# Seven-product pairs of blocks without GpSimd: products in another order, summed in PSUM over copies, in operations twice as wide

## The chip, the cores and the metric

The kernel runs on one core of a Trainium2 chip. The metric is the device time of one execution in microseconds (us), shown as the median of several runs. One execution was also taken by the hardware profiler; where the text says "the profiled execution", it means that one.

## The reference

All inputs are float32; B = 8 sequences, 8 heads, S = 576 positions, 64 features per head, so rows of 512 features. What is computed, cut to what matters:

```python
kv  = einsum('bhsd,bhse->bhde', k, v)          # per head, 64 x 64
out = einsum('bhsd,bhde->bhse', q, kv)         # linear attention without softmax
x   = out / sqrt(mean(out**2, -1) + 1e-6) * g_norm     # then heads side by side: [8, 576, 512]
u   = x + ((x^T @ U) @ V)^T                    # U [576, 32], V [32, 576]: mixes positions
y   = u + relu(u @ w_ch1) @ w_ch2              # [512, 2048] and [2048, 512]
```

U, V and the two large weights come as float64 and are decoded to float32 on the chip.

## The kernel before

**Blocks.** The 8 x 576 = 4608 rows of u are held transposed and cut into nine blocks of 512 columns. Blocks 0 to 2 go through the two large products directly: for each of 16 chunks f of the 2048 hidden features, `ffn1` makes one 128x512 tile h, `relu` makes its two parts hh and hl, and `ffn2` adds into four PSUM banks y. To keep float32 accuracy on the fast matmul, every operand is split into a high part (a rounding copy, on ScalarE) and a low part (source minus high part, on VectorE); a product is three matmuls, high by high, high by low, low by high.

**Pairs.** Blocks 3 to 8 go as three pairs (q = 0, 1, 2). A pair is a 2x2 block problem, done with seven products P1 to P7 instead of eight. `UNITS` lists 112 units of six 128x512 matmuls for each pair: 28 units of a *first stage* (`first_unit`: four groups g of h, seven products each), 28 units of a *second stage* (`second_unit`: seven products, four units each, summing over g), and the same again for the other half of the hidden features. So a pair has four stages, first, second, first, second, and there are twelve stages in all.

**What feeds the stages.** `factor` makes the right-hand operands of the first stage (sums and differences of blocks, then split). `weight_combos` makes the weights of all seven products during blocks 1 and 2, 16 calls in all, and puts them in DRAM (`wd`), from where `load_units` fetches four units at a time. In the first stage the sums of P1, P6 and P5 are copied to SBUF (`spare`, L635), P7, P3, P4 and P2 are added to them on VectorE (L638) and rectified on ScalarE (L639), and GpSimd makes the combinations of h that the second stage needs (L641, L642, L662, L664). In the second stage `make_part` splits a combination into hh (ScalarE, L659) and hl (VectorE, L660) up to three units ahead of the unit that uses it; the results are added to x on VectorE (L693, L695) and, from the copies, on GpSimd (L689). GpSimd also does the sums inside `weight_combos` (L571, L579) and the differences in `factor` (L545).

**Attention beside it.** While PE works on one block or pair, the attention of later sequences is prepared in steps of one head pair each: `kv_step`, `out_step`, `stats_step`, `mul_step`, `xsplit_step`, `turn_step`, `t_step`, `t4_step`, `mix_part`. `STARTS`, `PARTS`, `STARTS2` and `EARLY` say behind which unit each step stands.

**Order.** PE's order is that of the program from block 2 on; before that, and on the other engines throughout, a scheduler places the instructions when the program is built. Every engine takes its queue in order. All DMAs are issued by SyncE (SP).

Of the kernel before, what the change touches and what calls it, by code (L numbers as in the profile page):

```python
# [82 lines left out]
def build(ctx: ExitStack, tc: tile.TileContext, kv_in, kvt0_in, kvt_in, q_in, uv_in, g_in, w_in, out):  # L83
# [152 lines left out]
    def decode_w(f):  # L236
# [9 lines left out]
        def low_half():  # L246
            w = got["w"]
            nc.vector.tensor_tensor(out=w[:, 1], in0=t, in1=w[:, 0].bitcast(F32), op=ALU.subtract)
# [16 lines left out]
    def bank():  # L265
        bank_no[0] += 1
        if startup[0] and bank_no[0] % (7 - NEARLY) >= 3 - NEARLY:
            return ps_y.tile([P, 512], F32, name="y")
        return ps_p.tile([P, 512], F32, name="pp")

    def low_bank(b):
        return ps_h.tile([P, 512], F32, name="h") if b > 4 else bank()
# [862 lines left out]
```

## Time and profile before

| what | value |
|---|---|
| time, median of 3 runs | 924.05 us (923.7 to 924.52) |
| profiled execution, its own time | 923.1 us |
| span of its instructions | 921.1 us |
| busy, TensorE (PE) | 864.7 us, 94% |
| busy, VectorE (DVE) | 671.2 us, 73% |
| busy, ScalarE (ACT) | 463.1 us, 50% |
| busy, GpSimd (POOL) | 357.8 us, 39% |
| first matmul of the pairs | at 374.3 us |

PE, DVE, ACT, POOL and SP are TensorE's matmuls, VectorE, ScalarE, GpSimd and SyncE; PEld is TensorE's loading of weights. A row of a group reads: line, engine, operation, output and inputs, shapes, count, then busy time in us and the mean of one in ns, then how long the engine sat idle before such instructions and what ended that. A matmul counts as busy for its whole latency, so a PE that is busy is not one at its peak.

### The profile page before, as it was taken

To read this page: it belongs to the slowest core of one execution; us is meant where nothing else is said; L and a number is where in the kernel's file an instruction comes from. 1 tells how busy PE (TensorE), PEld (TensorE's weight loads), DVE (VectorE), ACT (ScalarE), POOL (GpSimd) and SP (SyncE) were. 2 spreads that over 40 slices of the span, in tenths; PEclk is the share of its full clock that TensorE was granted. 3 is DMA by queue.
4 is the path that set the end of the run, shared out by engine and by line. 5 is a ranking of instruction groups with operands and counts; after the bars stand their busy time and mean duration, and the time that the engine had idled before them with its cause. 6 is when DMAs were issued, how large, how long until landed. Compare 5 with 4: busy or idle time off the path is not lost.

```text
span 921.1 us, 12302 instructions
## 1 busy us (share of the span) xinstructions
PE 864.7 (94%) x4196; PEld 704.4 (76%) x4196; DVE 671.2 (73%) x1099; ACT 463.1 (50%) x890; POOL 357.8 (39%) x301
## 2 busy tenths in 40 slices
PE   8899998989979999999899969998999699999998
PEld 7678876878868888887688747787887478878876
DVE  5798877666688566679786997369659973484496
ACT  5677733433334244455545835455457434553553
POOL 2000037566553002134242692137325932543491
PEclk9999999999989999999899989999999999999999
DMA  9989865535666462377568536765566367555553
GB/s 344 418 317 293 244 191 191 191 118 199 193 204 193 124 204 94 132 248 276 171 210 294 199 118 194 262 234 170 201 221 209 97 199 253 185 187 201 204 186 133
DMA packets 76670, 191.17 MB, mean 208 GB/s; under 512 B 8640, under 2 KB 38848, under 8 KB 65856
## 3 DMA queue, kind: packets, MB, share of 16 engines
q1 hardware_dynamic: 76608, 190.39, 61.3%
q8 instruction: 33, 0.54, 0.2%
q14 instruction: 29, 0.24, 0.1%
HBM read 143.30 MB, written 47.05 MB: 207 GB/s over the span
## 4 chain that ended last, share of the span: by engine, by line
PE 47%; DVE 17%; DMA 2%; issue 2%; ACT 1%; SPq 0%; POOL 0%; DVEq 0%; ACTq 0%
PE y L629 18%; PE y L678 15%; PE y L489 4%; DVE dec L660 4%; DVE hl L660 4%; DVE uc L554 2%; PE pp L312 2%; DVE hk L638 1%; PE pp L289 1%; PE h L475 1%; PE h L476 1%; PE h L477 1%; DMA out<-x 1%; DVE x L693 1%; DVE xt L370 1%
## 5 line engine op out<-in xcount | busy, mean ns | idle before, releaser
L629 PE MATMUL y<-uc,wt 128*128 128x512 f32 x966 | 229.9, 393 | 1.0 <-ACT sp L635 1.0
L629 PEld LDWEIGHTS y<-uc,wt 128*128 128x128 f32 x966 | 178.7, 188 | 37.9 <-ACT sp L635 1.4
L678 PE MATMUL y<-dec,wt 128*128 128x512 f32 x504 | 128.8, 399 | 1.4 <-DVE dec L660 0.7
L678 PEld LDWEIGHTS y<-dec,wt 128*128 128x128 f32 x504 | 94.2, 191 | 27.9 <-DVE dec L660 9.0
L489 PE MATMUL y<-hh,ws 128*128 128x512 f32 x336 | 113.6, 399 | 1.8 <-ACT hh L481 1.7
L678 PE MATMUL y<-hh,wt 128*128 128x512 f32 x336 | 114.0, 397 | 0.0
L638 DVE TENSOR_TENSOR hk<-y,sp 128x512 f32<-128x512 f32 x92 | 62.7, 688 | 68.6 <-PE y L629 56.2
L641 POOL TENSOR_TENSOR hk<-hk 128x512 f32<-128x512 f32 x24 | 31.6, 1316 | 184.4 <-ACT hk L639 184.4
L689 POOL TENSOR_TENSOR x<-x,sp 128x512 f32<-128x512 f32 x48 | 75.6, 1598 | 68.3 <-DVE x L695 55.2
L639 ACT ACTIVATE hk<-hk 128x512 f32<-128x512 f32 x96 | 60.3, 630 | 52.9 <-DVE hk L638 51.6
L678 PE MATMUL y<-hl,wt 128*128 128x512 f32 x168 | 68.2, 406 | 15.6 <-DVE hl L660 15.2
L660 DVE TENSOR_TENSOR hl<-hk,hh 128x512 fp32r<-128x512 f32 x72 | 72.9, 1027 | 12.9 <-ACT hh L659 12.0
L660 DVE TENSOR_TENSOR dec<-hk,dec 128x512 fp32r<-128x512 f32 x72 | 67.6, 946 | 9.0 <-ACT dec L659 8.9
L678 PEld LDWEIGHTS y<-hh,wt 128*128 128x128 f32 x336 | 64.2, 191 | 12.8
L489 PEld LDWEIGHTS y<-hh,ws 128*128 128x128 f32 x336 | 62.0, 188 | 15.3 <-ACT hh L481 3.1
L475 PE MATMUL h<-ut,ws 128*128 128x512 f32 x168 | 67.0, 399 | 5.1 <-DVE hl L482 5.1
L476 PE MATMUL h<-ut,ws 128*128 128x512 f32 x168 | 66.3, 394 | 0.0
L477 PE MATMUL h<-ut,ws 128*128 128x512 f32 x168 | 66.3, 394 | 0.0
L635 ACT COPY sp<-y 128x512 f32<-128x512 f32 x69 | 40.3, 585 | 51.6 <-PE y L629 51.2
L659 ACT CAST hh<-hk 128x512 fp32r<-128x512 f32 x72 | 44.7, 621 | 42.7 <-PE y L678 29.5
L489 PE MATMUL y<-hl,ws 128*128 128x512 f32 x168 | 65.9, 392 | 0.0
L579 POOL TENSOR_TENSOR dec<-dec 128x256 f32<-128x256 f32 x64 | 48.9, 784 | 33.2 <-DMA wd<-dec 26.1
(227 smaller groups left out, 1619.6 us busy)
## 6 DMA issues: line engine op xcount, KB each, us to landing
wt<-wd SPq DMA_DIRECT2D x84, 1024.0 KB, 4.9
kv_sb<-kv_in SPq DMA_DIRECT2D x29, 512.0 KB, 4.3
raw<-w_in SPq DMA_DIRECT2D x14, 1023.6 KB, 15.0
wd<-ws SPq DMA_DIRECT2D x84, 128.0 KB, 3.1
q_sb<-q_in SPq DMA_DIRECT2D x29, 288.0 KB, 3.4
wd<-sh SPq DMA_DIRECT2D x32, 256.0 KB, 3.3
wd<-dec SPq DMA_DIRECT2D x32, 256.0 KB, 3.8
ut<-xd SPq DMA_DIRECT2D x28, 288.0 KB, 3.6
```

Of the source, the lines that this page charges most:

```text
L475: nc.tensor.matmul(h, lhsT=w1s[f][0][:, d, :], rhs=uh[d], start=(d == 0), stop=False)
L476: nc.tensor.matmul(h, lhsT=w1s[f][0][:, d, :], rhs=ul[d], start=False, stop=False)
L477: nc.tensor.matmul(h, lhsT=w1s[f][1][:, d, :], rhs=uh[d], start=False, stop=(d == ND - 1))
L489: nc.tensor.matmul(acc, lhsT=w2s[f][w][:, c, :], rhs=h[:, cols], start=(f == 0 and w == 0 and h is hh), stop=(f == NF - 1 and w == 1))
L579: nc.gpsimd.tensor_tensor(out=o, in0=a, in1=b, op=op)
L629: nc.tensor.matmul(acc, lhsT=w[:, ws_, e * P:(e + 1) * P], rhs=u[:, us], start=fresh and e == 0 and n == 0, stop=e == 1 and n == 2, skip_g ...
L638: nc.vector.tensor_tensor(out=to, in0=acc, in1=other, op=ALU.add)
L639: nc.scalar.activation(out=to, in_=to, func=AF.Relu)
L659: nc.scalar.copy(out=hh, in_=src)
L660: nc.vector.tensor_tensor(out=hl, in0=src, in1=hh.bitcast(F32), op=ALU.subtract)
L678: nc.tensor.matmul(acc[c], lhsT=w[:, ws_, c * P:(c + 1) * P], rhs=h, start=fresh and kk == 0 and i == 0, stop=kk == KEEP - 1 and i == 2, s ...
L689: nc.gpsimd.tensor_tensor(out=to, in0=to, in1=s, op=ALU.add)
```

## The change

What it does:

- **No GpSimd in the pairs, nor in `weight_combos`, `factor` or the hand-over of block 2's rest.** The combinations of h, the sums of weights and the differences of blocks are made on VectorE (`less`). The rest of block 2 goes through DRAM (`sided`).
- **Operations on 1024 elements.** A product's two neighbouring units write one tile of two PSUM banks (`pair_bank`: z for P1 and P2, x for P5 and P3, y for P6, P7 and P4). Copies, sums, rectifiers, combinations, `factor` and the final sums each work on both at once. The attention of b > 4 gets banks of its own (`h`, `big`).
- **Sums in PSUM.** The order is P1 P5 P6 P2 P7 P3 P4 in both stages. P1's sum is copied by ScalarE from bank z to bank y, and P6, P7 and P4 accumulate there one upon the other; P2 accumulates on P1 in z, P3 on P5 in x. Only P5 and P6 are still kept in SBUF.
- **Weights.** From chunk 8 on, the decoded weights are also stored to DRAM (`wf`) and read back by `weight_combos`; the earlier ones are summed from their parts on VectorE. The quarters that need no sum are stored by `weight_quarters`, 48 DMAs of 256 KB in place of 96 of 128 KB. The 16 calls of `weight_combos` stand behind given relus (`COMBOS`): ten in block 1, six in block 2.
- **Attention.** Its starts are spread to one head pair per 11 units (`STARTS`, `PARTS`); kvb is copied on ScalarE instead of reduced on VectorE; for b > 4 the raw result is copied out of PSUM, squared from SBUF and scaled in SBUF.
- **Factors of the next pair** stand behind given units (`MAKE`, `after_unit`).

The diff, cut to its core:

```diff
-STARTS = {5: (2, 9, 16, 23), 6: (32, 44, 56, 64), 7: (8, 18, 56, 66)}
+COMBOS = [(1, f) for f in (1, 2, 4, 5, 7, 8, 10, 11, 13, 14)] + [(2, f) for f in (2, 4, 5, 7, 8, 10)]
+STARTS = {5: (0, 11, 22, 33), 6: (44, 55, 66, 77), 7: (3, 14, 25, 36)}
...
-USE = "P1 P6 P5 P7 P3 P4 P2".split()
-USE2 = "P2 P1 P6 P5 P7 P3 P4".split()
+USE = "P1 P5 P6 P2 P7 P3 P4".split()
...
+        if f >= 2 * FROM_DRAM:
+            last = steps["D2"]
+            steps["D2"] = lambda: (last(), nc.sync.dma_start(out=wf[f // 2][:, :, f % 2], in_=t))
...
-                nc.vector.tensor_reduce(out=kb[own, own], in_=parts[own, own], axis=AX.X, op=ALU.add)
+            move("kv", p if b == 0 else -1, kb[own, own], pp[own, own])
...
-        for k in range(2):
-            nc.gpsimd.tensor_tensor(out=r[:, k], in0=whole(2 * i + k, n, 0).bitcast(F32), in1=whole(2 * i + k, n, 1).bitcast(F32),
-                                    op=ALU.add)
+        if i < FROM_DRAM:
+            for k in range(2):
+                nc.vector.tensor_tensor(out=r[:, k], in0=whole(2 * i + k, n, 0).bitcast(F32),
+                                        in1=whole(2 * i + k, n, 1).bitcast(F32), op=ALU.add)
+        else:
+            nc.sync.dma_start(out=r, in_=wf[i][:, n])
...
-            nc.gpsimd.tensor_tensor(out=o, in0=a, in1=b, op=op)
+            nc.vector.tensor_tensor(out=o, in0=a, in1=b, op=op)
...
+    def pair_bank(name):
+        which = dict(P1="z", P2="z", P5="x", P3="x").get(name, "y")
+        return once(("bank", which), lambda: second_y[which].tile([P, 2, BLK], F32, name="yy"))
+    def keep_sum(name):
+        acc = pair_bank(name)
+        last["unit"] = nc.scalar.copy(out=pair_bank("P6") if name == "P1" else spare(name), in_=acc)
+    def less(out, a, b):
+        nc.vector.tensor_tensor(out=out, in0=a, in1=b, op=ALU.subtract)
...
-        nc.vector.tensor_tensor(out=to, in0=acc, in1=other, op=ALU.add)
-        nc.scalar.activation(out=to, in_=to, func=AF.Relu)
-        if name == "P2":
-            nc.gpsimd.tensor_tensor(out=h12, in0=h22, in1=h12, op=ALU.subtract)
-            nc.gpsimd.tensor_tensor(out=kept_t(g), in0=h12, in1=h11, op=ALU.add)
+        to, other = dict(P2=(h11, None), P7=(h22, "P5"), P3=(h12, "P6"), P4=(h21, None))[name]
+        if other:
+            nc.vector.tensor_tensor(out=to, in0=acc, in1=spare(other), op=ALU.add)
+        last["unit"] = nc.scalar.activation(out=to, in_=to if other else acc, func=AF.Relu)
+        if name == "P3":
+            at_stage(q, n + 1, lambda: less(kept_t(g), h12, h11))
+            at_stage(q, n + 4, lambda: less(h12, h22, h12))
...
-            nc.gpsimd.tensor_tensor(out=to, in0=to, in1=s, op=ALU.add)
+        if other:
+            nc.vector.tensor_tensor(out=y, in0=y, in1=spare(other), op=ALU.add)
```

How the order moves, at three places. First POOL's queue at the end of a pair. Before, the last pair's first and second stage stand there as follows (hk are the kept h, t a combination of them, x the block that becomes the output, sp a copied sum):

```order
L641 TENSOR_TENSOR hk<-hk 128x512 x2
L642 TENSOR_TENSOR t_3902<-hk 128x512
L662 TENSOR_TENSOR hk<-hk,t_3902 128x512
L664 TENSOR_TENSOR hk<-hk,t_3902 128x512 x2
L689 TENSOR_TENSOR x_2631<-x_2631,sp 128x512 x2
L689 TENSOR_TENSOR x_2632<-x_2632,sp 128x512 x2
```

Now POOL's queue ends in block 1, with the decoded V and block 0's outputs:

```order
masks.py:199 AFFINE_SELECT ident<-ident 128x128
L833 CAST v_92<-uvs 32x144 x12
L520 TENSOR_TENSOR st<-st,ut 128x512 x4
L1150 UNCONDITIONAL_BRANCH
L1150 ISA
```

All of POOL's rows behind block 1 are gone.

Second, DVE in the last pair. Before, a first stage has sixteen sums of 512 elements (L638), with the second stage's low parts (L660) behind them:

```order
L638 TENSOR_TENSOR hk<-y,sp 128x512 x6
L660 TENSOR_TENSOR dec<-hk,dec 128x512
L638 TENSOR_TENSOR hk<-y,sp 128x512 x2
L660 TENSOR_TENSOR dec<-hk,dec 128x512
L638 TENSOR_TENSOR hk<-y,sp 128x512
L660 TENSOR_TENSOR hl<-hk,hh 128x512 x2
L695 SCALAR_TENSOR_TENSOR x_2631<-x_2631,g_sb,y 128x512
```

Now it has four sums of 1024 (L681) and the combinations, which are `less` (L660 is now the line of that helper, so low parts and combinations share it):

```order
L681 TENSOR_TENSOR hk<-yy,sp 128x1024 x2
L660 TENSOR_TENSOR t_3650<-hk 128x1024
L660 TENSOR_TENSOR hk<-hk 128x1024
L660 TENSOR_TENSOR hk<-hk,t_3650 128x1024
L660 TENSOR_TENSOR dec<-hk,dec 128x512 x2
L681 TENSOR_TENSOR hk<-yy,sp 128x1024 x2
L660 TENSOR_TENSOR t_3506<-hk 128x1024
L660 TENSOR_TENSOR hk<-hk,t_3506 128x1024
```

Combinations now stand in DVE's queue among the low parts for which PE waits.

Third, DVE in block 1, where PE waits for hl of each chunk (L482 before, L504 now). Before, between two of them:

```order
L482 SCALAR_TENSOR_TENSOR hl<-h,hh 128x512
L585 TENSOR_TENSOR sh<-dec,sh 128x2x256
L585 TENSOR_TENSOR dec<-dec 128x2x256
L462 TENSOR_TENSOR ut_86<-pp,ut_86 128x384
L462 TENSOR_TENSOR ut_86<-pp,ut_86 128x192
L421 SCALAR_TENSOR_TENSOR ut<-ut_86,g_sb,ut 128x384
```

And now, at the same steps of the attention (L612 and L621 are the sums of weights, L627 their low parts):

```order
L504 SCALAR_TENSOR_TENSOR hl<-h,hh 128x512
L621 TENSOR_TENSOR dec<-dec 128x256
L627 TENSOR_TENSOR sh<-dec,sh 128x2x256
L481 TENSOR_TENSOR ut_86<-pp,ut_86 128x384
L627 TENSOR_TENSOR dec<-dec 128x2x256
L481 TENSOR_TENSOR ut_86<-pp,ut_86 128x192
L612 TENSOR_TENSOR dec<-ws_601 128x512
L612 TENSOR_TENSOR dec<-ws_649 128x512
L440 SCALAR_TENSOR_TENSOR ut<-ut_86,g_sb,ut 128x384
```

The sums of weights, which stood in POOL's queue, now stand between hl and hl, and L621, which overwrites the buffer of the call before, is in DVE's queue behind that call's DMAs.

More of the change, by code (lines that the diff above doesn't have):

```diff
@@ new lines, in place, with factor, diff @@
+    def place(name):
+        return once(("u", name), lambda: const.tile([P, 2, 2, BLK], F32R, name="uc", tag=f"w_{2 + USE.index(name)}"))
+    def factor(q, names, es=slice(0, 2)):
+        x11, x12, x21, x22 = [t[:, es, n * BLK:(n + 1) * BLK] for t in x32_tiles(q) for n in range(2)]
+        t = st[:, es]
+        def diff(a, b, t=t):
+            less(t, a, b)
+            return t
+        plans = dict(P1=lambda: x11, P3=lambda: x22, P2=lambda: x21, P5=lambda: diff(x12, x11),
+                     P6=lambda: diff(x22, t), P4=lambda: diff(x21, t), P7=lambda: diff(x22, x12, kept_t(2)[:, es]))
@@ L557, in build @@
+            nc.vector.scalar_tensor_tensor(out=lo, in0=src, scalar=g_sb, in1=hi.bitcast(F32), op0=ALU.mult, op1=ALU.subtract)
+    w_tile = {}
+    wf = [tc.dram_tile([P, 2, 2, DM], F32, name=f"wf{i}") for i in range(NG)]
     wd = [tc.dram_tile([P, 4, 2, 2 * P], F32, name=f"wd{i}") for i in range(NU // 4)]
@@ L586, in weight_combos @@
             for k, name in enumerate(names):
-                put(name, None, both[:, k])
-        for name, (k, m) in (("P1", quarter[0]), ("P2", quarter[1]), ("P4", quarter[3])):
-            for s in range(2):
-                put(name, s, whole(2 * i + k, n, s)[:, m * HALF:(m + 1) * HALF])
+                nc.sync.dma_start(out=store(name, n, i), in_=both[:, k].bitcast(F32))
     coming = {}
@@ L646, in make_part @@
+    last, parts = {}, {}
     def make_part(q, n):
@@ L671, in second_unit @@
         final = g >= KEEP
-        m = USE2.index(name) % 2
-        acc = [y2(2 - 2 * m + c) for c in range(2)]
-        fresh = name in ("P1", "P2", "P6")
+        acc = pair_bank(name)
         hh, hl = parts.pop((q, n))
@@ L713, in second_unit @@
-        (r, half), s = dict(P2=((0, 0), None), P3=((0, 1), s6), P7=((1, 1), s15), P4=((1, 0), s1))[name]
-        for c in range(2):
-            plus_bank(y(r, c, half), acc[c])
-            if name != "P2":
-                if not final:
-                    plus(y(r, c, half), s[:, c])
-                done(r, c, half)
+        if name in ("P1", "P5", "P6"):
+            keep_sum(name)
+            return
+        (r, half), other = dict(P2=((0, 0), None), P7=((1, 1), "P5"), P3=((0, 1), "P6"), P4=((1, 0), None))[name]
@@ L991, in build, with after_unit @@
     for q in range(PAIRS - 1):
-        made = [(names, e) for names in ("P1", "P5 P6 P4", "P7", "P3", "P2") for e in range(2)]
-        for i, (names, e) in enumerate(made):
-            at_stage(q, MAKE[0] + MAKE[1] * i, lambda q=q, names=names, e=e: factor(q + 1, names, e))
-    last = {}
+        for at, names in MAKE[q]:
+            at_stage(q, at, lambda q=q, names=names: after_unit(lambda: factor(q + 1, names)))
+    def after_unit(what):
+        with tc.issue_after(last["unit"].ins):
+            what()
     def in_block(j, f, what):
@@ L1058, in build @@
         y_prev = y
+    ffn2(y_prev, [hprev])
+    finish(y_prev, NC - 1)
+    first_y.close()
+    for name in "y x z big".split():
+        second_y[name] = ctx.enter_context(tc.tile_pool(name=f"ps_{name}", bufs=1, space=bass.MemoryType.PSUM))
     for q in range(PAIRS):
```

300 lines of the change are left out of this document (144 added, 156 removed).

## The prediction

> **What bounds the kernel now.** I read the page first, then busy time by stage, then the operations that PE waits for. The page:
>
> ```profile
> span 921.1 us, 12302 instructions
> PE 864.7 (94%) x4196; PEld 704.4 (76%) x4196; DVE 671.2 (73%) x1099; ACT 463.1 (50%) x890; POOL 357.8 (39%) x301
> PE 47%; DVE 17%; DMA 2%; issue 2%; ACT 1%; SPq 0%; POOL 0%; DVEq 0%; ACTq 0%
> ```
>
> PE is the bound, and DVE is the only other engine with much of the chain that ended last. POOL has 39% busy time and none of the chain; the question is whether it costs time through others. PE's waits name DVE:
>
> ```profile
> PE y L678 <- DVE hl L660: 15.2, 8, 3.8
> PE h L475 <- DVE hl L482: 9.5, 6, 4.0
> ```
>
> Busy time by stage (columns: length, then PE, PEld, DVE, ACT, POOL with counts, granted clock, DMA share, GB/s). The first three rows are blocks 0 to 2, the others stages of the pairs: q=0 first, q=0 second, q=0's other second stage, q=1's other second stage, and the four stages of q=2:
>
> ```profile
> 28.80:155.00 126.20, 118.62 (x587) 95.92 (x586) 107.14 (x197) 77.93 (x123) 20.10 (x21) 1.00 0.80 267
> 155.00:268.50 113.50, 105.10 (x515) 86.23 (x514) 76.50 (x139) 43.49 (x98) 65.11 (x68) 0.97 0.57 182
> 268.50:374.26 105.76, 102.70 (x546) 86.60 (x545) 76.69 (x152) 42.48 (x96) 25.78 (x24) 0.98 0.49 154
> 374.26:427.09 52.83, 51.94 (x279) 43.41 (x278) 39.24 (x83) 29.34 (x63) 11.18 (x9) 1.00 0.69 236
> 427.09:480.02 52.93, 48.47 (x243) 39.77 (x242) 44.38 (x80) 27.51 (x60) 20.87 (x15) 0.94 0.61 207
> ...
> 526.17:576.75 50.58, 43.22 (x170) 32.03 (x168) 43.79 (x43) 23.70 (x41) 32.52 (x20) 0.93 0.50 161
> ...
> 708.91:761.08 52.17, 42.07 (x171) 30.66 (x170) 46.02 (x44) 24.01 (x41) 33.09 (x21) 1.00 0.50 156
> 761.08:797.97 36.89, 36.89 (x164) 30.57 (x163) 12.58 (x19) 17.60 (x29) 10.26 (x8) 1.00 0.70 236
> 797.97:838.20 40.23, 40.13 (x175) 32.41 (x175) 31.99 (x34) 20.09 (x34) 22.92 (x15) 1.00 0.52 183
> 838.20:874.93 36.73, 36.73 (x164) 30.41 (x163) 12.48 (x19) 17.65 (x29) 12.79 (x10) 1.00 0.57 200
> 874.93:917.50 42.57, 41.95 (x174) 31.61 (x173) 36.27 (x35) 20.05 (x34) 26.07 (x17) 1.00 0.45 161
> ```
>
> A stage has 28 units of six matmuls. First stages of q=2, which have no attention beside them, take 36.89 and 36.73 us: 36.8 us is PE's floor for a stage, 0.219 us a matmul. The first stage of q=0 has four head pairs beside it and twelve matmuls of block 2: (52.83 - 36.8 - 2.6) / 4 = 3.35 us of PE for a head pair. The floor of the pairs is so 12 x 36.8 + 2.6 + 12 x 3.35 = 484.4 us; they take 917.5 - 374.3 = 543.2 us. **58.8 us are lost**, nearly all in second stages: about 9.1 (427 to 480, less 2.1 head pairs by `STARTS`), 13.8, 15.4, 3.4 and 5.8 us in the five rows above, 11 in the rest.
>
> Why there: the low parts, min/median/max in ns, with a row of the first-stage sums for comparison:
>
> ```profile
> L660 DVE TENSOR_TENSOR hl<-hk,hh x72: 676/692/1778, 396.5 to 909.7; 128x512 fp32r<-128x512 f32 x72
> L660 DVE TENSOR_TENSOR hl<-t,hh x12: 681/1762/1780, 440.5 to 886.4; 128x512 fp32r<-128x512 f32 x12
> L660 DVE TENSOR_TENSOR dec<-t,dec x12: 685/1774/1782, 443.8 to 889.8; 128x512 fp32r<-128x512 f32 x12
> L638 DVE TENSOR_TENSOR hk<-y,sp x92: 669/692/693, 390.1 to 876.3; 128x512 f32<-128x512 f32 x92
> ```
>
> The same subtraction takes 0.69 us or 1.77; the sum with an input in PSUM never takes more than 0.693. The timeline in block 1 shows what makes the difference:
>
> ```profile
> 196.95 2.53 POOL L571 TENSOR_TENSOR dec<-ws 128x512 f32<-128x512 f32 x2 [1.46 <-DVE dec L585]
> 197.10 1.17 DVE L332 TENSOR_TENSOR ta<-r,half 128x10 f32<-128x10 f32 x1
> 198.30 1.20 DVE L333 TENSOR_TENSOR ta<-ta,r 128x10 f32<-128x10 f32 x1
> 201.35 0.50 PE L475 MATMUL h<-ut,ws 128*128 128x512 f32 x1 [2.38 <-DVE hl L482]
> 204.07 0.63 PE L477 MATMUL h<-ut,ws 128*128 128x512 f32 x1
> ```
>
> Two products of ten elements take 1.2 us each, as long as the POOL operations beside them: DVE with two inputs in SBUF stands still while POOL works. PE then idles 2.38 us, and its matmuls run slow for a while (0.63 us).
>
> **The change part by part.** Prices, mean ns behind the bar:
>
> ```profile
> L248 DVE TENSOR_TENSOR ws<-dec,ws 128x1024 fp32r<-128x1024 f32 x14 | 17.0, 1216 | 1.5 <-ACT ws L244 1.4
> L244 ACT CAST ws<-dec 128x1024 fp32r<-128x1024 f32 x14 | 14.7, 1048 | 6.1 <-DVE dec L150 6.1
> L635 ACT COPY sp<-y 128x512 f32<-128x512 f32 x69 | 40.3, 585 | 51.6 <-PE y L629 51.2
> L300 DVE TENSOR_REDUCE kvb<-pp 64x64 f32<-64x128 f32 x48 | 13.8, 287 | 0.6
> L462 DVE TENSOR_TENSOR x<-pp,ut x12: 424/446/458, 273.3 to 367.3; 128x288 f32<-128x288 f32 x8, 128x256 f32<-128x256 f32 x4
> L579 POOL TENSOR_TENSOR dec<-dec 128x256 f32<-128x256 f32 x64 | 48.9, 784 | 33.2 <-DMA wd<-dec 26.1 <-DVE ws L248 5.8
> ```
>
> *Second stages.* With POOL silent, a low part costs 0.69 us. DVE has 28 of them (19.3 us), four combinations and six final sums of 1024 elements at 1.22 (12.2 us): 31.5 us in PE's 36.8. For comparison, it is busy 43.8 and 46.0 us in the two worst stages now. A head pair's attention costs DVE at most (39.24 - 12.58) / 4 = 6.7 us, from the two first stages with and without it. The first second stage of q=0 now has a head pair per 11 units, 2.5 in it: DVE 31.5 + 16.8 = 48.3 against PE's 36.8 + 8.4 = 45.2, so 3 us lost, and 4 with gaps. Its other one has about 1.2 head pairs and, late, two factors with their differences (8.0 + 4.9): 44.4 against 40.8, again 4. The first one of q=1 has 2.1 head pairs, 45.6 against 43.8: 3. Its other one has three factors and two differences, 37.6 against 36.8: 1. Those of q=2 have DVE at 31.5: 1 for both. Lost: 13 us.
>
> *First stages.* DVE has four sums and four combinations, 9.8 us of 36.8. What is new is the chain in PSUM: P1's copy must be in bank y before P6 starts, P6's copied out before P7 starts, and P7's read before P4. Between each there is one product of two units, 12 x 0.219 = 2.6 us. ScalarE's copy of 1024 from PSUM to PSUM is not in the trace; 1.05 (L244, from SBUF) and 2 x 0.585 = 1.17 (L635) bound it; I take 1.1, nearer to L635 because of the same source. That leaves 1.5 us, which covers one attention operation ahead of it in ScalarE's queue, and not two. I charge 5 us for the six first stages; without any cover, a copy late by 1 us would cost that once for each of 12 groups and 6 second stages, 18 us.
>
> So the pairs lose 13 + 5 = 18 us in place of 58.8: **40.8 us gained**.
>
> *Blocks 1 and 2.* DVE takes over 16 sums of 512 (0.69) and 64 of 256, which lie at 0.42 to 0.46 (L462): 11.0 + 28.5 = 39.5 us. It loses 24 reductions of L300, 6.9 us, to ScalarE, which is not half busy. So 76.5 + 76.7 + 32.6 = 185.8 us in 219.3, 85%. Queued behind them is hl, for which PE waits; the two matmul groups of `ffn2` cover 2.6 us of it. Against that, PE's idle time in block 1, 8.4 us, comes partly from POOL's hold on DVE. I take 3 us better for block 1 and 4 worse for block 2, where DVE had more room and six calls now stand; the ends are 8 better and, below, 35 worse.
>
> *Block 0 and the end.* The decode's buffer is held until its store to DRAM has landed; half a MB takes 4.3 us to land, the last column of the list of DMAs, against 1.05 + 1.22 us of splitting which it overlaps:
>
> ```profile
> kv_sb<-kv_in SPq DMA_DIRECT2D x29, 512.0 KB, 4.3
> ```
>
> DVE is 85% busy there, so some of the 2 us show: 2 worse. SP issues 48 DMAs fewer, on no path. At the end, the last sum covers both banks and starts after the last matmul rather than three matmuls earlier: 0.6 worse.
>
> Sum: 921.1 - 40.8 - 3 + 4 + 2 + 0.6 = 883.9 us of span. The profiled execution's own time is 2.0 us over its span, 923.1, and 0.95 under the median of 924.05, so it stands for the runs. Forecast: **886 us**, and 877 to 904 with the 18 us of the pairs halved or doubled.
>
> **The rivals.** *DVE becomes the bound of the second stages* (0.20). For it: two rows of DVE's waits for ScalarE there, which a queue kept in order may not fill:
>
> ```profile
> L660 DVE TENSOR_TENSOR hl<-hk,hh 128x512 fp32r<-128x512 f32 x72 | 72.9, 1027 | 12.9 <-ACT hh L659 12.0
> L660 DVE TENSOR_TENSOR dec<-hk,dec 128x512 fp32r<-128x512 f32 x72 | 67.6, 946 | 9.0 <-ACT dec L659 8.9
> ```
>
> If these 21.9 us all come onto the path, 908 us. Against it: in q=2 DVE has 5 us of room in each stage.
>
> *More is gained* (0.13): POOL's hold also made the idle time of block 1, block 2 costs nothing (-9 us), and the pairs lose 7 us rather than 18: 866 us.
>
> *The slowness is not POOL's* (0.02): the low parts keep their mean of 0.95 to 1.03 us, DVE needs 28 x 0.99 + 12.2 = 39.9 us in each second stage, and with the attention the loss stays near 60: 924 us, no change. The row that L638 gives (PSUM input, never slow) speaks against it. The Trainium skill, "SBUF — State Buffer", section "SBUF: two separate sides", has a lock: a VectorE operation with two SBUF inputs and a GpSimd operation that reads SBUF exclude each other for a whole instruction; by that rule this rival is empty, and the trace agrees as far as L332 and L638 go.
>
> *Slower: the weights' sums stop DVE in blocks 1 and 2* (0.05). L579 waited 26.1 us in all for DMAs of the call before, while POOL stood. The same wait now stands in DVE's queue, with hl behind it, and PE behind hl. DVE's path there is 185.8 + 26.1, and the waits for ScalarE that it has already come on top:
>
> ```profile
> L482 DVE SCALAR_TENSOR_TENSOR hl<-h,hh 128x512 fp32r<-128x512 f32 x48 | 32.7, 682 | 31.2 <-ACT hh L481 30.8
> L585 DVE TENSOR_TENSOR sh<-dec,sh 128x512 fp32r<-128x512 f32 x16 | 11.3, 707 | 11.2 <-ACT sh L584 11.1
> 200.00:210.00 10.00, 8.65 (x42) 7.18 (x42) 7.34 (x14) 3.35 (x7) 5.43 (x6) 0.83 0.41 113
> ```
>
> With 30.8 + 11.1 that is 253.8 us against 219.3, 34.5 more; and if each of 14 such waits brings the dip of the last row (clock 0.83 over 10 us, 1.7 us), 24 more: 886 + 58 = 944 us. It ends slower once the two blocks together grow by more than 39 us over my sum. Against it: the 26.1 us came from calls that followed at once, and now most stand two or three chunks apart. The Trainium skill, "TensorE: Matmul & The Clock Gate", Part 1, has the clock drop only after an idle window of about 3.4 us; by that rule 2.4 us gaps would cost no clock, and this rival would end near 920. The row above, after 2.38 us of idle time, decides for the dip.
>
> **How the numbers follow.** Chances: forecast 0.60, the others as given. A measurement of this kernel can tell 0.2%, 1.9 us, from no change. Faster: 0.60 + 0.20 + 0.13 = 0.93; same 0.02; slower 0.05. The range leaves out the last two rivals (0.07), the worse third of the first (0.07) and the better half of the second (0.06): 865 to 910 us.
>
> **What would show it.** Right: no low part above 0.75 us; second stages of q=2 at 37 to 38 us and those of q=0 under 49; the pairs in about 502 us; blocks 1 and 2 within 8 us of 219. Wrong: PE waiting for ScalarE's copies into bank y (the PSUM chain), hl waiting behind sums of weights whose release is a DMA (the slower rival), or low parts still at 1.7 us with POOL idle.

## The result and the profile after

The kernel after takes **881.04 us** (median of 4 runs, 879.51 to 882.06), the kernel before beside it 924.28 us (4 runs, 923.7 to 926.47). The ratio is **0.9527, 95% interval 0.9506 to 0.9548**: 4.7% faster. The profiled execution has a span of 879.5 us against 921.1, 41.6 us less.

The page of the kernel after: GpSimd is nearly idle (11.8 us, of which 6.7 ahead of block 0 and 5.2 in block 1), VectorE has 60 us less work, and TensorE has 67% of the chain that ended last, where it had 47%.

```profile
span 879.5 us, 11845 instructions
PE 849.5 (97%) x4220; PEld 705.4 (80%) x4220; DVE 611.4 (70%) x1085; ACT 456.2 (52%) x830; POOL 11.8 (1%) x33
PE 67%; DVE 13%; DMA 11%; ACT 3%; issue 3%; SPq 2%; POOL 0%; DVEq 0%; ACTq 0%; POOLq 0%
PE yy L717 25%; PE yy L669 24%; PE y L511 5%; DMA dec<-wf 3%; DMA wd<-dec 3%; PE h L494 2%; DVE dec L621 2%; PE h L495 2%; PE h L496 2%; DMA ut<-xd 1%; PE h L300 1%; PE big L319 1%; DMA xd<-xt 1%; SPq L629 1%; DMA kvq<-kv_in 1%
```

The two DMAs in that chain, 3% each, are new in the chain: loads of decoded weights, and stores of weight combinations, in blocks 1 and 2.

Busy time by stage in the kernel after, same columns as in the prediction. The first three rows are blocks 0 to 2, cut where the rectifier of a block's first chunk starts (the last one ends at block 2's last chunk); then q=0's two second stages, q=1's other second stage, and the first two stages of q=2.

```profile
34.75:150.33 115.58, 109.76 (x543) 88.59 (x544) 94.34 (x184) 71.63 (x114) 0.00 (x0) 1.00 0.92 292
150.33:257.77 107.44, 103.26 (x516) 85.55 (x515) 77.88 (x171) 42.57 (x101) 5.17 (x4) 0.98 0.62 190
257.77:370.70 112.93, 104.19 (x561) 86.52 (x560) 81.86 (x185) 48.63 (x117) 0.00 (x0) 1.00 0.68 207
422.27:468.25 45.98, 45.98 (x246) 38.97 (x244) 40.21 (x72) 29.00 (x62) 0.00 (x0) 1.00 0.69 235
516.78:556.21 39.43, 39.43 (x182) 32.67 (x181) 33.92 (x51) 23.06 (x39) 0.00 (x0) 1.00 0.69 245
683.33:721.99 38.66, 38.39 (x170) 31.45 (x168) 34.80 (x42) 22.09 (x32) 0.00 (x0) 1.00 0.65 228
721.99:760.07 38.08, 38.08 (x170) 31.53 (x168) 12.29 (x13) 15.67 (x17) 0.00 (x0) 1.00 0.60 210
760.07:798.15 38.08, 38.08 (x170) 31.53 (x168) 27.42 (x34) 18.42 (x28) 0.00 (x0) 1.00 0.54 194
```

TensorE is busy without a break in nearly every stage. The four rows of second stages took 52.9, 50.6, 52.2 and 38.9 us before, cut at their first matmuls like these (the prediction's 40.23 for the last one begins about a unit early). Blocks 0 to 2 of the kernel before, cut at the same points:

```profile
34.36:149.48 115.12, 107.58 (x523) 87.15 (x524) 97.51 (x182) 73.33 (x113) 14.65 (x16) 1.00 0.81 269
149.48:265.05 115.57, 107.17 (x531) 88.04 (x530) 78.27 (x138) 44.70 (x101) 70.55 (x73) 0.97 0.56 177
265.05:371.64 106.59, 103.53 (x554) 87.37 (x554) 77.44 (x156) 42.85 (x98) 24.79 (x24) 0.98 0.51 159
```

So block 0 is 0.5 us longer, block 1 8.1 shorter, block 2 6.3 longer. These are single profiles: five of the kernels below (a_h_pool, a_narrow, a_old_starts, a_bunched, a_two_copies) have the same code in these blocks and took 115.6 to 118.5, 106.1 to 108.1 and 109.5 to 111.8 us there, so differences of some 3 us in one block show nothing. The pairs, from the first matmul of the first stage to the end of the last, go from 543.1 us (with 2.7 us of block 2 among them) to 498.6. They carry the whole gain. The low parts after, min/median/max in ns:

```profile
L660 DVE TENSOR_TENSOR hl<-hk,hh x72: 650/686/701, 391.0 to 867.1; 128x512 fp32r<-128x512 f32 x72
L660 DVE TENSOR_TENSOR dec<-hk,dec x72: 633/687/701, 413.1 to 870.2; 128x512 fp32r<-128x512 f32 x72
L660 DVE TENSOR_TENSOR hl<-t,hh x12: 682/688/693, 425.1 to 840.2; 128x512 fp32r<-128x512 f32 x12
```

None takes 1.77 us any more.

### The profile page after: what moved, and what is told of

The parts are those of the page before. It is cut to its first block, busy times and chain, and to the rows that moved or that the text cites. A ratio compares the mean times of both kernels' runs of the same rounds, so it can differ in the third digit from the quotient of the medians.

```text
span 879.5 us, 11845 instructions
## 1 busy us (share of the span) xinstructions
PE 849.5 (97%) x4220; PEld 705.4 (80%) x4220; DVE 611.4 (70%) x1085; ACT 456.2 (52%) x830; POOL 11.8 (1%) x33
## 4 chain that ended last, share of the span: by engine, by line
PE 67%; DVE 13%; DMA 11%; ACT 3%; issue 3%; SPq 2%; POOL 0%; DVEq 0%; ACTq 0%; POOLq 0%
PE yy L717 25%; PE yy L669 24%; PE y L511 5%; DMA dec<-wf 3%; DMA wd<-dec 3%; PE h L494 2%; DVE dec L621 2%; PE h L495 2%; PE h L496 2%; DMA ut<-xd 1%; PE h L300 1%; PE big L319 1%; DMA xd<-xt 1%; SPq L629 1%; DMA kvq<-kv_in 1%
## 5 line engine op out<-in xcount | busy, mean ns | idle before, releaser
L669 PE MATMUL yy<-uc,wt 128*128 128x512 f32 x1008 | 236.6, 392 | 0.0
L669 PEld LDWEIGHTS yy<-uc,wt 128*128 128x128 f32 x1008 | 187.1, 188 | 38.1
L717 PE MATMUL yy<-dec,wt 128*128 128x512 f32 x504 | 123.3, 391 | 0.3 <-DVE dec L660 0.3
L717 PE MATMUL yy<-hh,wt 128*128 128x512 f32 x336 | 112.2, 391 | 0.0
L717 PEld LDWEIGHTS yy<-dec,wt 128*128 128x128 f32 x504 | 93.7, 188 | 19.9 <-DVE dec L660 0.7
L660 DVE TENSOR_TENSOR dec<-hk,dec 128x512 fp32r<-128x512 f32 x72 | 49.0, 686 | 37.4 <-ACT dec L699 37.0
L660 DVE TENSOR_TENSOR hl<-hk,hh 128x512 fp32r<-128x512 f32 x72 | 48.4, 687 | 37.5 <-ACT hh L699 36.9
L717 PEld LDWEIGHTS yy<-hh,wt 128*128 128x128 f32 x336 | 63.1, 188 | 13.1
L717 PE MATMUL yy<-hl,wt 128*128 128x512 f32 x168 | 65.5, 390 | 0.0
L699 ACT CAST dec<-hk 128x512 fp32r<-128x512 f32 x72 | 44.3, 620 | 29.2 <-PE yy L717 15.4
L657 ACT COPY sp<-yy 128x1024 f32<-128x1024 f32 x36 | 36.5, 1015 | 35.3 <-PE yy L669 27.3
L621 DVE TENSOR_TENSOR dec<-dec 128x256 f32<-128x256 f32 x64 | 24.9, 419 | 34.9 <-DMA dec<-wf 18.1
L494 PEld LDWEIGHTS h<-ut,ws 128*128 128x128 f32 x168 | 32.0, 190 | 13.4 <-DVE hl L504 5.5
```

The source lines that it names most:

```text
L494: nc.tensor.matmul(h, lhsT=w1s[f][0][:, d, :], rhs=uh[d], start=(d == 0), stop=False)
L621: nc.vector.tensor_tensor(out=o, in0=a, in1=b, op=op)
L657: last["unit"] = nc.scalar.copy(out=pair_bank("P6") if name == "P1" else spare(name), in_=acc)
L660: nc.vector.tensor_tensor(out=out, in0=a, in1=b, op=ALU.subtract)
L669: nc.tensor.matmul(acc[:, i], lhsT=w[:, ws_, e * P:(e + 1) * P], rhs=u[:, e, us], start=name in ("P1", "P5") and e == 0 and k == 0, stop=e ...
L699: last["unit"] = nc.scalar.copy(out=hh, in_=src)
```

## The experiments

Two theories. **Silence**: GpSimd's hold on VectorE made the loss in the pairs, and it goes when GpSimd stops. **Structure**: the gain comes from VectorE's smaller load (sums in PSUM, wide operations) and from how its work is placed. All twelve runs, with the length of the pairs in their profiles (old order: less the 2.7 us of block 2). Each ratio is to the kernel before in the same comparison, which took 921.22 us in the one with b_pairs_dve, b_all_dve, a_h_pool and a_combos_pool, and 924.28 to 924.91 in the others. Across comparisons times and ratios agree to some 4 us only (a_combos_pool is 6 us above the kernel after by the ratios, 2 by the spans); the pairs agree within 0.2 us wherever they were left alone.

| kernel | time, us | ratio, 95% interval | pairs, us |
|---|---|---|---|
| before | 924.28 | 1 | 540.4 |
| after | 881.04 | 0.9527 (0.9506 to 0.9548) | 498.6 |
| b_pairs_dve | 907.61 | 0.9855 (0.983 to 0.988) | 524.5 |
| b_all_dve | 910.11 | 0.9875 (0.986 to 0.989) | 525.2 |
| b_spread | 910.88 | 0.9861 (0.9832 to 0.989) | 527.5 |
| a_h_pool | 890.67 | 0.967 (0.9644 to 0.9696) | 509.0 |
| a_combos_pool | 883.95 | 0.9594 (0.9575 to 0.9612) | 498.6 |
| a_narrow | 881.67 | 0.954 (0.9513 to 0.9566) | 500.2 |
| a_old_starts | 884.11 | 0.9563 (0.954 to 0.9585) | 500.0 |
| a_bunched | 886.51 | 0.96 (0.9572 to 0.9628) | 507.2 |
| a_two_copies | 880.28 | 0.9527 (0.9501 to 0.9552) | 498.6 |
| a_r_ahead | 882.75 | 0.9554 (0.953 to 0.9578) | 498.6 |
| a_no_dram | 870.59 | **0.9418** (0.9397 to 0.9439) | 498.5 |
| a_no_dram_even | 871.38 | 0.9434 (0.9412 to 0.9455) | 498.6 |

**b_pairs_dve: GpSimd silent in the pairs, all else old.** The same edit at L545, L641, L642, L662, L664 and L689:

```diff
-            nc.gpsimd.tensor_tensor(out=h12, in0=h22, in1=h12, op=ALU.subtract)
+            nc.vector.tensor_tensor(out=h12, in0=h22, in1=h12, op=ALU.subtract)
```

> The kernel before with one thing altered: the 168 GpSimd operations of the pairs (combinations of h, differences in factor, sums into x) stand on VectorE, still 512 elements wide, in the old order of products and with the old copies. Theory (GpSimd's hold on VectorE made the loss): low parts all at 0.69 us; a second stage needs 28 low parts, 8 combinations, 8 sums from PSUM and 8 sums from SBUF, 52 x 0.69 = 35.9 us of VectorE in 38.1 of TensorE, so most of the loss goes: 885 to 900 us. Rival (the width of the operations and the sums in PSUM made the gain): 116 us more on VectorE in place of GpSimd stop TensorE at least as much as before: 915 us or more.

Measured 0.9855: 15.9 us less in the pairs, between the two theories; 15.5 of them are in the six second stages. Its low parts:

```profile
L660 DVE TENSOR_TENSOR hl<-hk,hh x72: 675/692/698, 396.5 to 893.2; 128x512 fp32r<-128x512 f32 x72
L660 DVE TENSOR_TENSOR dec<-t,dec x12: 645/688/699, 440.5 to 876.0; 128x512 fp32r<-128x512 f32 x12
```

The hold is gone to the last one, and the four stages of q=2 take 38.1 to 38.2 us each. In q=0 and q=1 TensorE still waits. Its worst wait in the pairs, 3.12 us at 538 to 541.1 us, as VectorE's timeline shows it (start, duration):

```profile
536.03 0.76 DVE L554 SCALAR_TENSOR_TENSOR uc<-st,g_sb,uc 128x512 fp32r<-128x512 f32 x1
536.70 0.69 DVE L662 TENSOR_TENSOR hk<-hk,t 128x512 f32<-128x512 f32 x1
537.30 0.75 DVE L554 SCALAR_TENSOR_TENSOR uc<-st,g_sb,uc 128x512 fp32r<-128x512 f32 x1
537.96 0.70 DVE L664 TENSOR_TENSOR hk<-hk,t 128x512 f32<-128x512 f32 x1
538.56 0.70 DVE L545 TENSOR_TENSOR st<-x,x 128x512 f32<-128x512 f32 x1
539.16 0.70 DVE L664 TENSOR_TENSOR hk<-hk,t 128x512 f32<-128x512 f32 x1
539.76 0.70 DVE L662 TENSOR_TENSOR hk<-hk,t 128x512 f32<-128x512 f32 x1
540.36 0.70 DVE L660 TENSOR_TENSOR hl<-t,hh 128x512 fp32r<-128x512 f32 x1
```

The low part that TensorE waits for (540.36) stands behind factors and combinations, with no pause in the queue: VectorE is the bound at this wait, not because it is held but because too much comes at once. Silence alone, net of the work that VectorE takes over, is worth 15.9 of 41.8 us.

**b_all_dve: the weights' sums on VectorE too.** L571 and L579 altered like the lines above.

> As the run named before it, and the sums of weights in blocks 1 and 2 on VectorE too (32 of 512 elements, 64 of 256, about 49 us), at the old places and without the load from DRAM. Theory: block 1 gains what GpSimd's hold cost there and loses what the sums cost, so 5 us either way from the run before it. Rival (the weights' sums stop VectorE): 20 us or more above it, in blocks 1 and 2.

2.5 us above b_pairs_dve, as the first theory had it: blocks 0 to 2 take 113.5, 117.8 and 107.1 us against 115.6, 114.9 and 106.6. In the old placing, some 49 us of sums (by the expectation) cost some 3 us net in blocks 1 and 2: releasing VectorE there pays for nearly all of them, and gains nothing.

**a_h_pool: the combinations of h back on GpSimd.**

```diff
-    def less(out, a, b):
-        nc.vector.tensor_tensor(out=out, in0=a, in1=b, op=ALU.subtract)
+    def less(out, a, b, eng=nc.vector):
+        eng.tensor_tensor(out=out, in0=a, in1=b, op=ALU.subtract)
...
+            less(h11[:, gs], h22[:, gs], kept_t(g), nc.gpsimd)
```

> The kernel after with the 48 combinations of h back on GpSimd, 1024 elements wide, everything else as it is. Theory: low parts of up to 2.4 us come back in the second stages, where a combination of about 2.4 us of GpSimd work lies beside them, and TensorE waits for hl again: 15 to 30 us more than the kernel after, 896 to 911. Rival (width and PSUM made the gain): VectorE is relieved of 48 x 1.22 = 59 us and the time stays at 878 to 884 or falls.

10.4 us more in the pairs, though VectorE has 48 operations less: under the 15 to 30 of the first theory, but far from the rival's none. The low parts and GpSimd's combinations:

```profile
L660 DVE TENSOR_TENSOR hl<-hk,hh x72: 651/684/2889, 388.5 to 875.1; 128x512 fp32r<-128x512 f32 x72
L660 DVE TENSOR_TENSOR dec<-hk,dec x72: 634/684/2898, 410.6 to 878.2; 128x512 fp32r<-128x512 f32 x72
L660 POOL TENSOR_TENSOR hk<-hk x24: 2367/2570/3499, 397.5 to 863.1; 128x1024 f32<-128x1024 f32 x24
```

A low part now lasts up to 2.9 us: its own 0.69 and nearly a whole GpSimd operation on 1024 elements (2.4 us at least, 2.6 in the middle). The hold is shown from both sides: taken away in the old kernel, put back in the new one. The 10.4 us need not all be the hold's, though: a combination also takes twice as long on GpSimd (2.4 us against 1.22), so a low part's source comes later. In q=1's last stage, 4.0 us longer than in the kernel after, both show: GpSimd's first combination ends at 693.55 us, ScalarE can only then make the high part, and the two low parts behind it take 5.11 us together. The two were not tried apart. The Trainium skill, "SBUF — State Buffer", section "SBUF: two separate sides", has a VectorE operation with two inputs in SBUF and a GpSimd operation that reads SBUF exclude each other for a whole instruction; these rows agree, since the hold doubled with the width.

**a_combos_pool: the weights' sums back on GpSimd.** L612 and L621 with `nc.gpsimd` for `nc.vector`.

> The kernel after with the sums of weight_combos in blocks 1 and 2 (16 of 512 elements, 64 of 256) back on GpSimd, pairs as they are. Theory (GpSimd's hold costs block 1 more than the sums cost): block 1 grows by about 6 us, block 2 shrinks by about 4, 881 to 885 us. Rival (what costs in block 2 is that VectorE's queue waits for the DMAs of the decoded weights): those waits go to GpSimd's queue, block 2 gives back its 6 us and block 1 stays, 873 to 877 us.

Blocks 0 to 2 take 115.2, 112.0 and 111.1 us, against 115.6, 107.4 and 112.9: block 1 grows by 4.6, near what the first theory said; the 1.8 us less in block 2 are within what single profiles differ by. So over half of the 8.1 us that block 1 gained come from VectorE being free of GpSimd there. The rival's cause is not excluded by this run, because the wait was moved and not taken away: GpSimd now waits 69.4 us for the loads in seven waits, ScalarE waits for GpSimd's sums, and VectorE's low parts behind them (L627) wait 33.2 us for ScalarE.

**a_narrow: no operation on 1024 elements.** Copies, sums, rectifiers, combinations, factors and final sums each in a loop:

```diff
-            nc.vector.tensor_tensor(out=to, in0=acc, in1=spare(other), op=ALU.add)
+            for i in range(2):
+                nc.vector.tensor_tensor(out=to[:, i], in0=acc[:, i], in1=spare(other)[:, i], op=ALU.add)
```

> The kernel after with every operation on 1024 elements in the pairs cut into two of 512 (copies, sums, rectifiers, combinations, factors, final sums), same queues and order. Two operations of 0.69 us take the place of one of 1.22 on VectorE, two of 0.59 that of one of 1.02 on ScalarE: some 12 % more of the part of VectorE's time that is wide. Theory (GpSimd's silence and the placing of the work made the gain, VectorE has room): 0 to 4 us above the kernel after, ratio 0.953 to 0.957. Rival (the width made what GpSimd's silence alone did not bring): most of 28 us come back, ratio 0.97 or more.

0.954; the pairs take 1.6 us more. In this structure, where VectorE has room, width is nearly all spare.

**a_old_starts: attention of sequences 5 and 6 at the old units.**

```diff
-STARTS = {5: (0, 11, 22, 33), 6: (44, 55, 66, 77), 7: (3, 14, 25, 36)}
+STARTS = {5: (2, 9, 16, 23), 6: (32, 44, 56, 64), 7: (3, 14, 25, 36)}
...
-                at_stage((b - 5) // 2, start + PARTS[at], what)
+                at_stage((b - 5) // 2, start + (PARTS if b == 7 else PARTS2)[at], what)
```

> The kernel after with the attention of sequences 5 and 6 at the starts and steps of before (a head pair per 7 units at first, then per 8 to 12), everything else as it is. Theory (the bunching of VectorE's work made what was left when GpSimd alone was silenced): the two first stages of the pairs lose 5 to 12 us, with waits for the attention's sums or for low parts that the kernel after does not have: ratio 0.958 to 0.966. Rival (the banks of their own and the narrower queue make the starts irrelevant): within 2 us of the kernel after, ratio 0.951 to 0.955.

0.9563, just outside the rival's range, and a miss for the first theory: the first two stages do grow by 5.3 us, but the next two shrink by 3.9, because the same head pairs now stand in other stages. The pairs take 1.4 us more, no 5 to 12.

**a_bunched: old starts for sequence 7 too, and the factors at the old units.**

```diff
-STARTS = {5: (0, 11, 22, 33), 6: (44, 55, 66, 77), 7: (3, 14, 25, 36)}
+STARTS = {5: (2, 9, 16, 23), 6: (32, 44, 56, 64), 7: (8, 18, 56, 66)}
...
-        for at, names in MAKE[q]:
-            at_stage(q, at, lambda q=q, names=names: after_unit(lambda: factor(q + 1, names)))
+        made = [(names, e) for names in ("P1", "P5 P6 P4", "P7", "P3", "P2") for e in range(2)]
+        for i, (names, e) in enumerate(made):
+            at_stage(q, 86 + 2 * i, lambda q=q, names=names, e=e: factor(q + 1, names, slice(e, e + 1)))
```

> The kernel after with the attention of sequences 5 to 7 at the old starts and steps, and the factors of the next pair at the old units, 86 to 104, 512 elements wide and not held behind a unit's operations. GpSimd stays silent, sums stay in PSUM. Theory (bunches of work on VectorE): the second stages that carry factors and head pairs lose 3 to 8 us each, the pairs take 508 us or more in place of 498.6, ratio 0.964 or more. Rival (sums in PSUM, wide operations and the banks leave VectorE room for the bunches): the pairs take 503 us or less, ratio 0.958 or less.

507.2 us in the pairs, 8.6 more: between the two, nearer to the first theory. But the second stages with the factors, which it named, lose next to nothing: the fourth and eighth stage take 38.7 and 38.2 us. With the same factors at the same units they took 50.6 and 52.2 us in the kernel before, and 46.6 and 45.2 in b_pairs_dve, where GpSimd was silent too. In the new structure VectorE has room for that bunch; there the second theory is right. What TensorE waits for in the pairs is the attention:

```profile
PE big L319 <- DVE ts L419: 2.8, 2, 1.6
PE big L474 <- ACT t L423: 2.6, 1, 2.6
PE yy L717 <- DVE hl L660: 0.3, 1, 0.3
```

**b_spread: the new places in the old structure.** b_pairs_dve with

```diff
-STARTS = {5: (2, 9, 16, 23), 6: (32, 44, 56, 64), 7: (8, 18, 56, 66)}
-MAKE = 86, 2
...
+STARTS = {5: (0, 11, 22, 33), 6: (44, 55, 66, 77), 7: (3, 14, 25, 36)}
+PARTS = dict(kv=0, out=5, turn=9, xsplit=9, t=14, mix0=19, mix1=21)
+MAKE = ((74, 76, 99, 101, 104, 106, 103, 107, 86, 90), (75, 77, 85, 88, 92, 95, 99, 102, 105, 108))
```

> The kernel before with GpSimd's work in the pairs on VectorE (as in the first experiment), and in addition the attention of the pairs at the starts of the kernel after (one head pair per 11 units) and the factors of the next pair spread over 33 units rather than 18; order of products, width and copies stay the old ones. Theory (what silence alone did not bring was lost to bunches of work on VectorE, with hl behind them): the pairs fall from 527 us to 505 to 512, ratio 0.962 to 0.972. Rival (it takes the sums in PSUM, the new order of products or the attention's own banks): the pairs stay at 520 or more, ratio 0.980 or more.

The pairs stay at 527.5 us, as the rival said, but partly for another reason: the fourth stage grew from 46.6 to 56.0 us by one new wait of 9.5 us, for a copy on ScalarE. The other eleven stages together are 6.3 us shorter, some of it attention that moved into the fourth.

```profile
PE h L386 <- ACT xh L168: 12.6, 3, 9.5
PE y L679 <- DVE dec L661: 6.5, 4, 3.3
PE h L388 <- DVE xl L180: 3.5, 3, 2.7
```

So the new places bring 6.3 us in eleven stages of the old structure. The 9.5 us belong to this variant, whose other operations were not moved to match; what it would do without them stays open, and so this run does not settle what places are worth there.

**a_two_copies: P1's copy in PSUM made twice.**

```diff
-        last["unit"] = nc.scalar.copy(out=pair_bank("P6") if name == "P1" else spare(name), in_=acc)
+        for _ in range(2 if name == "P1" else 1):
+            last["unit"] = nc.scalar.copy(out=pair_bank("P6") if name == "P1" else spare(name), in_=acc)
```

> The kernel after with each copy of P1's sum from bank to bank made twice, one behind the other on ScalarE, so that bank y is ready about 1.0 us later in each of 12 groups of the first stages and in 6 second stages. If the chain in PSUM has 1.6 us to spare (two units of 1.36 us less a copy of 1.0): 0 to 3 us above the kernel after, ratio 0.953 to 0.957. If it has none, as a part of the forecast's 5 us for the first stages supposed: 12 to 18 us, ratio 0.965 to 0.973.

Nothing: 0.9527, and the pairs take 498.6 us as before the edit. The copy costs what the prediction took (here x36, in the kernel after x18), and the chain has room for two:

```profile
L658 ACT COPY yy<-yy x36: 997/997/1017, 378.2 to 841.6; 128x1024 f32<-128x1024 f32 x36
```

**a_r_ahead: the load of decoded weights one call earlier.** The lines stand behind the last stores of `weight_combos`:

```diff
+        n2, i2 = (1, i) if n == 0 else (0, i + 1)
+        if FROM_DRAM <= i2 < NG:
+            nxt = ahead_r[n2, i2] = dec.tile([P, 2, DM], F32, name="dec")
+            nc.sync.dma_start(out=nxt, in_=wf[i2][:, n2])
```

> The kernel after with each load of decoded weights issued at the end of the call of weight_combos before, into the buffer that falls free there, instead of at the start of its own call. Theory (VectorE's queue stands still until that load lands, and hl and the attention stand behind it): block 2, 6.3 us longer than before the change, gives back 4 to 8 us: ratio 0.944 to 0.949. Rival (the waits are hidden and VectorE's work itself, 40 us more, makes block 2 longer): within 2 us, ratio 0.951 to 0.955.

0.9554, at the upper end of the rival's range, but it doesn't settle the question, because the edit did not take the waits away: the stores ahead of the load were late themselves, the load was issued only 6.8 us before the sum could start, and VectorE's waits for these loads grew from 18.1 us in the kernel after to 24.7. Block 2 gave back 4.2 us (108.7), and block 1 lost 5.4 (112.8). The third load of block 2 and its use, from SyncE's and VectorE's timelines (two answers):

```profile
308.29 0.56 SPq L634 DMA_DIRECT2D dec<-wf  x1
```

```profile
315.08 0.76 DVE L622 TENSOR_TENSOR dec<-dec 128x256 f32<-128x256 f32 x2 [3.06 <-DMA dec<-wf]
```

**a_no_dram: no load at all.** `FROM_DRAM = 8` in place of 4.

> The kernel after with all weights summed from their parts on VectorE and none stored to and read back from DRAM (16 sums of 512 elements more, 11 us of VectorE; 16 loads of 1 MB and 8 stores less). If VectorE's waits for those loads (18.1 us, of which some stand on the path in block 2) cost more than the sums: 2 to 6 us below the kernel after, ratio 0.946 to 0.951. If VectorE's own work is the limit in blocks 1 and 2: 2 to 8 us above it, ratio 0.955 to 0.962.

**0.9418, better than either kernel** and below its range. (The expectation is wrong on the loads: they are eight of 0.5 MB, as the stores are.) Blocks 0 to 2 (same cut):

```profile
34.42:145.32 110.90, 106.78 (x525) 87.57 (x526) 91.82 (x180) 70.45 (x111) 0.00 (x0) 1.00 0.83 258
145.32:256.82 111.50, 105.78 (x534) 88.72 (x533) 85.03 (x183) 43.04 (x104) 5.95 (x4) 0.97 0.57 174
256.82:360.06 103.24, 102.74 (x561) 86.69 (x561) 87.39 (x194) 48.97 (x118) 0.00 (x0) 1.00 0.65 205
```

Block 2 gives back 9.7 us though VectorE has more to do there (87.4 us against 81.9), block 0 gives 4.7 without the stores, block 1 takes 4.1. So the load, not VectorE's work, cost block 2 its time; whether by VectorE's wait for it or by its traffic beside the other transfers was not tried apart.

**a_no_dram_even: that, with eight calls in each block.**

```diff
-COMBOS = [(1, f) for f in (1, 2, 4, 5, 7, 8, 10, 11, 13, 14)] + [(2, f) for f in (2, 4, 5, 7, 8, 10)]
+COMBOS = [(1, f) for f in (1, 3, 5, 7, 9, 11, 13, 15)] + [(2, f) for f in (1, 3, 4, 6, 7, 9, 10, 12)]
```

> The variant without the store and the load of decoded weights, with the 16 calls of weight_combos spread as eight in block 1 and eight in block 2, in place of ten and six. If block 1, now the longer of the two at 111.5 us against 103.2, is crowded by the calls: it gives back 3 us and block 2 takes 1 of them, ratio 0.938 to 0.941. If a call costs the same in either block: within 2 us of that variant, ratio 0.940 to 0.944.

0.9434: a call costs the same in either block (108.9 and 105.6 us against 111.5 and 103.2).

## Why the prediction was right, point by point

**The sum.** Forecast 886 us, measured 881.04. By the spans: predicted 883.9, measured 879.5.

**The bound and the size of the loss: a wrong term.** "36.8 us is PE's floor for a stage" is too low. The prediction cut those stages about one unit short: its windows hold 164 matmuls, whole stages 170 (168 and two at the edges). A whole stage takes 38.08 us (the two last rows of the table by stage above; the same first stages of the kernel before take that too), 0.2267 us a matmul. The eight stages of q=0 and q=1 in the kernel after, which have all twelve head pairs beside them, summed:

```profile
sum 346.11, PE 344.34 PEld 288.55 DVE 252.05 ACT 204.74 POOL 0.00; mean PE 43.04 PEld 36.07 DVE 31.51 ACT 25.59 POOL 0.00
```

TensorE's 344.3 us less 8 x 38.08 = 304.6 leave 39.7 / 12 = 3.31 us for a head pair, as predicted (3.35). The floor is 12 x 38.08 + 12 x 3.31 = 496.7 us. Lost before: 540.4 - 496.7 = 43.7, not 58.8. Lost after: 498.6 - 496.7 = 1.9, not 18. Both terms were 15 to 16 us too large, so that the difference of 41.8 came out as 40.8. That this was so near is luck in good part: the low floor stands in both terms, but most of the second came from VectorE's prices and from a charge for the chain in PSUM, and they have nothing to do with the first.

**Second stages: 13 us forecast, nearly nothing lost.** VectorE's prices were durations; its queue moves faster. In the timeline of b_pairs_dve low parts and combinations of 0.70 us start 0.60 us apart, and in that of the kernel after combinations of 1.22 us start 1.14 us apart (761.16 and 762.30 us). So 28 low parts and ten wide operations need an estimated 28 x 0.60 + 10 x 1.14 = 28.2 us back to back, not 31.5. (The table's 27.42 us are for 24 low parts and ten wide operations: four low parts stand in the stage before.) The Trainium skill, "Perfetto Trace Analysis", section "Optimizing Scalar/DVE Operations", says that part of an operation's shown latency overlaps the next instruction; the trace agrees, by 0.10 us of 0.70. In q=0's first second stage VectorE was busy 40.2 us, not 48.3, of 46.

**First stages: 5 us forecast for the chain in PSUM, none lost.** The copy took 1.0 us (1.1 forecast), and twice that costs nothing. TensorE never waits for it in the kernel after: of the 1.9 us that the pairs lose, 1.5 are two waits for the attention's sums (ts, L419) and 0.3 one wait for a low part.

**Why the loss went: a right mechanism, given too large a part.** The place, "nearly all in second stages", stands: the four second stages without attention took 50.6, 52.2, 38.9 and 41.1 us before, 30.4 of the 43.7 us over their floor. GpSimd's hold is shown as a mechanism (b_pairs_dve, a_h_pool). But silence alone brings 15.9 us; 8.6 us more are the places of attention and factors (a_bunched against after; its factors are also 512 wide); and 17.3 lie between b_pairs_dve and a_bunched, both without GpSimd and with the old places: 22.9 less in second stages, 5.6 more in first ones. The prediction named no other cause of the loss than the hold. One thing that differs there is VectorE's load, in the sums over the pairs: it is busy 396.54 us in the one and 334.26 in the other (331.35 in the kernel after).

```profile
sum 527.16, PE 506.95 PEld 416.03 DVE 396.54 ACT 282.44 POOL 0.00; mean PE 253.48 PEld 208.02 DVE 198.27 ACT 141.22 POOL 0.00
```

```profile
sum 507.21, PE 500.17 PEld 415.60 DVE 334.26 ACT 276.16 POOL 0.00; mean PE 55.57 PEld 46.18 DVE 37.14 ACT 30.68 POOL 0.00
```

That the smaller load made the 17.3 us is likely, and argued only. Width is worth 1.6 us by itself in the kernel after; in the old structure, where VectorE is short of time, it was not tried. How the 17.3 us divide among the sums in PSUM, the attention's own banks and the operations issued behind given ones was not tried apart, and stays open.

**Blocks.** Forecast +2, -3 and +4 us for blocks 0 to 2; measured +0.5, -8.1 and +6.3: signs right, and block 1 at the good end that was given. But block 2 is longer for another reason than the one forecast. The 4 us were charged for VectorE's added work; with more of that work and no loads, block 2 takes 103.2 us, less than before the change (a_no_dram). The load of decoded weights, on which the sum put nothing there, made it longer, so that the +4 came near by luck. And block 0's 2 us stood for the stores, but without them it takes 4.7 us less: something else gained some 4 us there, and no run shows what.

The mechanism of the slower rival, weights' sums that stop VectorE for a DMA, is real, but small. The wait that it named, for the stores of the call before, is 11.0 us in six waits in block 1, which became shorter all the same; and in a_no_dram, the fastest kernel, it is 20.8 us in 14 waits. In block 2 the wait is for the loads. These are VectorE's waits in the kernel after there, and the place of one:

```profile
DVE dec L621 <- DMA dec<-wf: 12.6, 5, 3.7
DVE dec L621 <- DMA ut<-xd: 3.4, 1, 3.4
```

```profile
326.92 1.56 DVE L621 TENSOR_TENSOR dec<-dec 128x256 f32<-128x256 f32 x4 [1.55 <-DMA dec<-wf]
```

Loads and stores together cost some 10 us (a_no_dram), where that rival had 58.

**The end.** 5.0 us from the last matmul to the end of the span, 3.9 before: 1.1 worse, 0.6 forecast.

**The rivals.** VectorE as the new bound: no, it has over 10 us of room in the second stages of q=2. More gained: no; the pairs lost less than it had, but block 2 did cost time. Slowness not GpSimd's: no, by the low parts, though GpSimd's silence alone brought only 15.9 us.

**The signs.** No low part of the pairs took more than 0.701 us, q=0's second stages took 46.0 and 39.4, the pairs 498.6 and blocks 1 and 2 together 220.4, all as named. Those of q=2 took 38.1 and 38.2 us, a little over the 37 to 38 named, because of the floor. One sign of being wrong showed as well: in block 2 sums of weights wait for a DMA.

## What to carry to other kernels

Take GpSimd off the buffers that VectorE works on before counting VectorE's time, but don't expect the whole loss to go with it: what was held then stands in one queue, and here the rest came only with less work in that queue and a better place for it. Avoid letting an engine that feeds the bound wait in its queue for a load that was issued a few us earlier; here making the data again (11 us of VectorE) was some 10 us cheaper than storing and fetching it. And measure a floor over a whole period, with its count of instructions beside it.

## What the hardware showed beside that

After the idle 3.12 us of b_pairs_dve, TensorE ran at half speed for over 4 us; after an idle 1.67 us it did not. (Idle time counts from the end of the matmul before, which the profile models.) From its timeline (x2 is two matmuls):

```profile
531.91 0.50 PE L678 MATMUL y<-hl,wt 128*128 128x512 f32 x1 [1.67 <-DVE hl L660]
532.25 0.62 PE L678 MATMUL y<-hh,wt 128*128 128x512 f32 x2
...
541.12 0.79 PE L678 MATMUL y<-hl,wt 128*128 128x512 f32 x1 [3.12 <-DVE hl L660]
541.71 1.05 PE L678 MATMUL y<-hh,wt 128*128 128x512 f32 x2
542.56 0.63 PE L678 MATMUL y<-hl,wt 128*128 128x512 f32 x1
542.99 1.05 PE L678 MATMUL y<-hh,wt 128*128 128x512 f32 x2
...
545.98 3.48 PE L678 MATMUL y<-dec,wt 128*128 128x512 f32 x12
```

Ten matmuls stand between 541.71 and 545.98, 0.427 us each against 0.227, so the dip cost 2 us on top of the wait. The Trainium skill, "TensorE: Matmul & The Clock Gate", Part 1, gives 426.7 ns from one matmul of 512 columns to the next with the clock halved, and the trace agrees; its idle window of about 3.4 us is longer than the 3.12 us that were enough here, and than the 2.38 us of the prediction's row.

The loads of decoded weights, 0.5 MB each, took 6.0 us from issue to landing (median of eight in the kernel after), the stores of the same size 4.4. The prediction took 4.3 us for the stores, which was right, and had no price for the loads.
